# Sixteen small copies moved from SyncE's queue to ScalarE's, in a fused attention and MLP kernel with a newly written order of emission

## The chip, the cores and the metric

The kernel runs on one core of a Trainium2 chip. The metric is the device time of one execution in microseconds, as the median of several runs. The profile is one execution taken by the hardware profiler; its times are microseconds from the first instruction.

## What is computed

```python
# attention, per batch and head (B=2, H=8, S=768, D=64)
k_sum = k.reshape(B, H, 24, 32, D).max(axis=3)
v_sum = v.reshape(B, H, 24, 32, D).mean(axis=3)      # the "value sums"
scores_l = scale * q @ k.T,  kept where |i - j| < 16, else -1e9
scores_s = scale * q @ k_sum.T + log(32)
a = softmax(concat([scores_l, scores_s]))
x = a @ concat([v, v_sum])                           # 1536 tokens x 512
# first MLP: 512 -> 2048 -> 512
h = relu(x @ w_in);  y = (h * h) @ w_out
# second MLP: 512 -> 1024 -> 512
h = y @ w2_in
solu = h * softmax(h)
out = (layernorm(solu) * g_ln) @ w2_out
```

All inputs and the output are float32.

## The kernel before

The program has three parts, and their work is interleaved. The attention is cut into sixteen units: four blocks of tokens (512, 256, 256 and 512 of them) times four pairs of heads. The first MLP runs in 54 steps; a step is one product with w_in (`mm1`, line 505, twelve matmuls), a relu, squares, and one product with w_out (`mm2`, line 537, twelve matmuls). The second MLP walks over twelve row blocks (lines 587 to 647). In both MLPs every float32 operand is split into a high and a low part, and three products replace one.

The emission order is a table written out by hand, `ORDER` (lines 21 to 59). Each token names a piece of work by a letter, an index and, where it can run on several engines, a last letter for the engine: `a` is ScalarE (ACT), `d` is VectorE (DVE), `p` is GpSimd (POOL). Every engine works through its own instructions in this order, so an instruction that waits holds up those behind it on its engine. SyncE (SP) issues the DMAs, also in that order. The pieces that matter here:

- `ls` (line 236) loads the values of one pair of heads into a `kl` buffer, laid out so that each of 96 partitions holds eight neighbouring rows. `y` (line 242) adds these eight rows in three additions of 512, 256 and 128 columns. `j` (line 249) is one matmul that adds four partitions and scales: that gives the 24 value sums of each of two heads. `J` copies them from PSUM to `vs`.
- `P` (`place_vs`, line 279) is a DMA that copies a unit's sums from `vs` to partitions 96 to 119 of the unit's value window `vw`, repeated for each of its blocks of 64 tokens. `lv` (lines 266 to 272) loads the values themselves into partitions 0 to 95. There are three windows, used in turn.
- `lk` (line 190) loads keys into a `kl` buffer too. `ls` and `lk` share two `kl` buffers, which are given out in the order of the table, so a load waits until the one two places earlier in that order has been read.
- `S` (line 316) makes scores, `R` (line 337, DVE) adds the mask and takes the maximum, `E` (line 345, ACT) the exponential, `n` and `N` (lines 350 to 355) normalise, `T` (line 361) transposes, `C` copies to SBUF (`pt`), and `V` (`att_v`, line 381) multiplies by the window `vw`. `V` needs both the load `lv` and the copy `P`. `H` (line 397, ACT) and `X` (line 94, DVE) split the result into `xh` and `xl`, on which `mm1` works.
- `K`, `Q` and `w` are copies of keys, queries and key windows (line 679 on ACT, line 676 on DVE, line 557 on POOL); `m` (line 207, DVE) is the maximum over 32 keys. `a` (line 437, ACT), `b`, `c`, `d`, `e` (lines 440, 444, 451, 454, DVE), `F` and `f` (line 94) prepare a tile of weights.
- `U`, `G` and `D` are the relu, the squares and the low part of a step; `D` stands in line 94 as `gl<-r,gh`.

The DMAs of the program signal their end on eight semaphores in turn, in the order of emission, whichever engine issues them (`DMAHW0` to `DMAHW7` below), and a DMA waits for the one that had its semaphore before.

The copy as it stands in the code:

```python
src = vs[b][32 * hp:32 * hp + NSUM]
nc.sync.dma_start(out=vw[u % NVB][WK:WN, b0:b0 + nb],
                  in_=src.unsqueeze(1).to_broadcast([NSUM, nb, P]))
```

Of the kernel before, what the change touches and what calls it, by code (L numbers as in the profile page):

```python
# [26 lines left out]
d3 e3 V2 T7 E8 ls4 l5 H2 n8 F3d P4 q5 f2d k12 K12a k13 Q5a S5 N8p X2 C7a V3 w6a a4 K13a R9 q6 b4 c4 H3 lq7 w7a T8 f3p
C8a lv5 Q6d y4p X3 S6 R10 l6 lq8 E9 n9 ls5 a5 d4 e4 M0 U0a b5 c5 N9d P5 j4 J4a q7 Q7d d5 V4 lv6 G0 D0p M1 H4 X4 m6 E10
n10 T9 l7 w8a F4a U1a e5 F5a C9a S7 O0 N10p q8 lk7 lq9 R11 E11 y5d f4d f5p V5 lv7 H5 P6 Q8d j5 J5d l8 lq10 a6 a7 X5 G1
ls6 T10 C10a lv8 b6 c6 d6 e6 F6a b7 S8 R12 w9a M2 n11 P7 N11d D1d l9 q9 Q9a k14 k15 K14a K15a T11 lq11 c7 d7 e7 f6p  # L30
w10a C11d S9 R13 O1 P8 E12 n12 a8 m7 F7a q10 Q10a N12p b8 c8 d8 U2a V6 H6 X6 V7 H7 X7 ls7 lv9 l10 T12 C12d f7p lq12 G2
# [24 lines left out]
f40p b44 c44 d44 e44 O49 M51 a45 F42d b45 c45 g44 G50 D50p Ya49 Yd49 O50 g43 U51d G51 d45 e45 g45 D51d F43d f41d f42p
z0 F44a F45a M52 U52a G52 O51 Z0d a46 b46 M53 c46 d46 e46 f43d f44d f45d U53a i0 D52d O52 l47 a47 G53 b47 c47 z1 Z1d
g46 F46a D53d d47 e47 g47 F47d f46p i1 f47p z2 Z2p u0 O53 Yd53 Ya53
"""


# [697 lines left out]
```

## Time and profile before

| | before |
|---|---|
| median of 3 runs | 501.98 us (500.7 to 502.87) |
| profiled execution | 504.72 us |
| its span, first to last instruction | 503.0 us |
| mean granted TensorE clock | 0.983 |
| busy: PE / DVE / ACT / POOL | 94% / 67% / 49% / 23% |
| first matmul of the first MLP | 58.15 us |
| last of the attention's splits (`X15`) | about 155 us |

The span is divided by stage: before the first product of the first MLP (attention alone, 58 us), the stretch in which attention and first MLP are mixed (to 155 us), the first MLP with weight preparation (to about 352 us), the passage to the second MLP (to 381 us), and the second MLP. "PEclk" is the TensorE clock that was granted, as a share of 2.4 GHz. In a chain of work each line is a piece that ended last and released the next; DMA issues stand under SPq, the SyncE's queue.

### The profile page before, as it was taken

The page shows a single profiled execution, that of the slowest core. Times are in us where ns is not written, and L with a number is a line of the kernel's source. Part 1 is how long each engine was busy: PE and PEld are TensorE (multiplying, and loading weights), DVE is VectorE, ACT ScalarE, POOL GpSimd, SP SyncE. Part 2 cuts the span into 40 slices and gives each one's busy share as a digit, 9 for nine tenths or more (in the row PEclk, how much of TensorE's full clock was granted, in tenths as well). Part 3 has the DMA queues.
Part 4 walks back from the last instruction along what each step waited for, and adds up shares of the span by engine and source line. Part 5 has one row for each costly group of instructions (what it writes and reads, how often), then busy time and mean ns, then how long its engine had stood idle before and what let it go on. Part 6 is the DMA issues. An engine that isn't in the chain of part 4 may idle for free.

```text
span 503.0 us, 8088 instructions
## 1 busy us (share of the span) xinstructions
PE 473.9 (94%) x2968; PEld 394.8 (78%) x2968; DVE 339.0 (67%) x756; ACT 247.9 (49%) x576; POOL 116.9 (23%) x134
## 2 busy tenths in 40 slices
PE   3686699999999999999999999999999999999997
PEld 2465477789999888888888888888877888888886
DVE  4777889875785459345237778986778787665560
ACT  3687688777764544435326536465522332222231
POOL 3255432721321331511022302101312112110000
PEclk9788899999999999999999999999999999999999
DMA  9999886486224122333011332330000010000011
GB/s 189 206 233 201 214 206 171 98 156 137 74 60 110 51 83 87 81 94 81 36 43 42 124 124 89 125 125 1 1 1 1 22 42 22 21 22 22 21 43 42
DMA packets 60359, 44.04 MB, mean 88 GB/s; under 512 B 46624, under 2 KB 49184, under 8 KB 60320
## 3 DMA queue, kind: packets, MB, share of 16 engines
q1 hardware_dynamic: 60320, 43.53, 34.9%
q8 instruction: 23, 0.38, 0.3%
q14 instruction: 16, 0.13, 0.1%
HBM read 39.19 MB, written 3.15 MB: 84 GB/s over the span
## 4 chain that ended last, share of the span: by engine, by line
PE 78%; DVE 7%; DMA 4%; issue 4%; POOL 3%; ACT 3%; SPq 2%; POOLq 0%; DVEq 0%; ACTq 0%
PE h L505 25%; PE acc L537 23%; PE po L647 13%; PE h L587 9%; DMA kl<-in_v_dram 2%; PE lt L624 2%; PE at L316 2%; PE at L381 1%; POOL kl L242 1%; DMA qr<-in_q_dram 1%; PE at L361 1%; DVE sm L337 1%; ACT sm L345 1%; DVE wf L444 1%; POOL sm L355 1%
## 5 line engine op out<-in xcount | busy, mean ns | idle before, releaser
L505 PE MATMUL h<-xh,wi 128*128 128x512 f32 (+1 forms) x432 | 131.9, 371 | 0.0
L537 PE MATMUL acc<-gh,wo 128*128 128x512 f32 (+1 forms) x432 | 130.2, 368 | 0.0
L505 PEld LDWEIGHTS h<-xh,wi 128*128 128x128 f32 x432 | 79.3, 190 | 14.5 <-issue 0.8
L537 PEld LDWEIGHTS acc<-gh,wo 128*128 128x128 f32 x432 | 78.7, 188 | 14.3 <-issue 1.0
L505 PE MATMUL h<-xl,wi 128*128 128x512 f32 (+1 forms) x216 | 79.5, 368 | 0.0
L537 PE MATMUL acc<-gl,wo 128*128 128x512 f32 (+1 forms) x216 | 79.2, 367 | 0.2 <-DVE gl L94 0.2
L587 PE MATMUL h<-w,wf 128*128 128x512 f32 x288 | 67.4, 390 | 0.5 <-DVE st L598 0.5
L587 PEld LDWEIGHTS h<-w,wf 128*128 128x128 f32 x288 | 54.0, 188 | 11.9 <-PE lt L624 0.7
L515 ACT ACTIVATE r<-h 128x512 f32<-128x512 f32 (+1 forms) x34 | 19.0, 559 | 63.7 <-PE h L505 62.6
L94 POOL TENSOR_TENSOR gl<-r,gh 128x512 fp32r<-128x512 f32 (+1 forms) x19 | 21.5, 1131 | 117.9 <-ACT r L524 103.4
L523 ACT ACTIVATE gh<-r 128x512 fp32r<-128x512 f32 (+1 forms) x54 | 31.3, 580 | 35.0 <-DVE r L517 26.8
L537 PEld LDWEIGHTS acc<-gl,wo 128*128 128x128 f32 x216 | 40.7, 188 | 7.1 <-DVE gl L94 0.7
L505 PEld LDWEIGHTS h<-xl,wi 128*128 128x128 f32 x216 | 41.0, 190 | 6.3
L94 DVE TENSOR_TENSOR gl<-r,gh 128x512 fp32r<-128x512 f32 (+1 forms) x35 | 25.8, 738 | 23.6 <-ACT r L524 21.8
L597 ACT ACTIVATE st<-h,nm 128x1024 f32<-128x1024 f32 x12 | 13.4, 1117 | 51.1 <-DVE nm L594 51.1
L454 DVE SCALAR_TENSOR_TENSOR wf<-st,wf 128x512 uint32<-128x512 uint32 x48 | 36.5, 763 | 1.0
L345 ACT ACTIVATE sm<-sm,mn 128x120 f32<-128x120 f32 x96 | 36.5, 383 | 0.5 <-DVE mn L337 0.4
L437 ACT ACTIVATE wf<-st 128x512 f32<-128x512 f32 x48 | 31.1, 660 | 8.9 <-DMA st<-in_moe_w_in_dram 6.4
L451 DVE SCALAR_TENSOR_TENSOR wf<-st,wf 128x512 uint32<-128x512 uint32 x48 | 34.3, 718 | 1.1
L524 ACT ACTIVATE r<-r 128x512 f32<-128x512 f32 (+1 forms) x54 | 31.6, 585 | 1.8
L440 DVE TENSOR_SCALAR wf<-wf 128x512 f32<-128x512 f32 x48 | 24.8, 518 | 11.1 <-ACT wf L437 11.0
L610 POOL TENSOR_TENSOR vr<-vr,mhalf 128x1 f32<-128x1 f32 x12 | 6.6, 550 | 105.0 <-DVE vr L609 105.0
(126 smaller groups left out, 755.6 us busy)
## 6 DMA issues: line engine op xcount, KB each, us to landing
st<-in_moe_w_out_dram SPq DMA_DIRECT2D x24, 512.0 KB, 3.4
st<-in_moe_w_in_dram SPq DMA_DIRECT2D x32, 256.0 KB, 4.2
st<-in_moe_w_in_dram SPq DMA_DIRECT2D x8, 512.0 KB, 4.0
kl<-in_v_dram SPq DMA_DIRECT2D x8, 384.0 KB, 4.2
kl<-in_k_dram SPq DMA_DIRECT2D x16, 192.0 KB, 4.5
out_dram<-ob SPq DMA_DIRECT2D x11, 256.0 KB, 2.0
vw<-in_v_dram SPq DMA_DIRECT2D x16, 168.0 KB, 3.9
qr<-in_q_dram SPq DMA_DIRECT2D x16, 128.0 KB, 5.0
```

What stands on the lines that cost most here:

```text
L94: eng.tensor_tensor(out=lo, in0=x, in1=hi.bitcast(F32), op=ALU.subtract)
L345: nc.scalar.activation(out=sm[:, j], in_=sm[:, j], func=AF.Exp, bias=mn[:, j:j + 1], scale=-1.0, accum_out=su[:, j:j + 1])
L437: nc.scalar.activation(out=wf_t[n], in_=st_t[n].rearrange("p (n t) -> p n t", t=2)[:, :, 1], func=AF.Abs)
L440: nc.vector.tensor_scalar(out=wf_t[n], in0=wf_t[n], scalar1=C_LO, scalar2=C_HI, op0=ALU.max, op1=ALU.min)
L451: nc.vector.scalar_tensor_tensor(out=w, in0=st[:, :, 0], scalar=29, in1=w, op0=ALU.logical_shift_right, op1=ALU.bitwise_or)
L454: nc.vector.scalar_tensor_tensor(out=w, in0=st[:, :, 1], scalar=0xC0000000, in1=w, op0=ALU.bitwise_and, op1=ALU.bitwise_or)
L505: nc.tensor.matmul(ps[:, 0:hi - lo], wi[:, wsel, d, :], x[t][:, d, lo:hi], start=(n == 0), stop=(n == 3 * HP - 1))
L523: nc.scalar.activation(out=gh, in_=r, func=AF.Square)
L524: nc.scalar.activation(out=r, in_=r, func=AF.Square)
L537: nc.tensor.matmul(acc_t[e][:, lo:hi], wo[:, wsel, e, :], x, start=(edge(s, -1, 3) and i == 0), stop=(edge(s, 1, 3) and i == 2))
L587: nc.tensor.matmul(h2[:, fs], x[:, c, :], w_t[NW1 + nh * NDC + c][:, wsel, :], start=(n == 0), stop=(n == 3 * NDC - 1))
L647: nc.tensor.matmul(po[:, ds], x[:, cs], w_t[NW1 + 8 + c][:, wsel, ds], start=(n == 0), stop=(n == 3 * NF2 - 1))
```

## The change

The DMA of line 279 is issued from ACT's queue instead of SP's: sixteen instructions. The table `ORDER` is written anew over its whole length (its two first lines stand here for it). Nothing else differs; what is computed and the number of pieces of work are the same.

```diff
 ORDER = """
-ls0 y0d j0 J0a lk0 k0 K0d l0 lq0 lk1 a0 k1 K1d m0 q0 w0a Q0a b0 c0 d0 e0 l1 F0a a1 S0 R0 E0 lq1 lk2 R1 E1 k2 k3 q1 ls1
-K2d K3d b1 n0 m1 lq2 k4 K4a N0p c1 k5 Q1d T0 lv0 lk3 lq3 lv1 K5d m2 w1a S1 y1p w2a f0d j1 C0d J1a q2 ls2 k6 R2 P0 E2
...
+ls0 lk0 lq0 l0 y0d j0 k0 J0d ls1 k1 lk1 K0a K1a q0 Q0a m0 y1d w0a l1 lq1 a0 S0 b0 j1 R0 E0 k2 lk2 K2d k3 K3a c0 d0 ls2
+e0 n0 m1 l2 lv0 J1a a1 R1 w1a N0p T0 b1 lq2 c1 d1 e1 q1 Q1a k4 k5 K4a y2p S1 C0d F0a F1a lk3 K5d m2 E1 w2p R2 R3 j2
...
@@ place_vs, line 279
             src = vs[b][32 * hp:32 * hp + NSUM]
-            nc.sync.dma_start(out=vw[u % NVB][WK:WN, b0:b0 + nb], in_=src.unsqueeze(1).to_broadcast([NSUM, nb, P]))
+            nc.scalar.dma_start(out=vw[u % NVB][WK:WN, b0:b0 + nb], in_=src.unsqueeze(1).to_broadcast([NSUM, nb, P]))
```

Three places show what moves.

**SP's queue** before the first MLP, before the change. It begins with the third load of values for sums (`kl<-in_v_dram`) and ends with the copy of unit 1's sums (`vw_107<-vs`); `vw_108` is the window of unit 2:

```order
L236 DMA kl<-in_v_dram 96x2x512 [waits DMAHW4_49,PE_49]
L279 DMA vw_106<-vs 24x8x128 [waits DMAHW5_49,Activation_49]
L190 DMA kl<-in_k_dram 128x6x64 [waits DMAHW6_49,PE_49]
L190 DMA kl<-in_k_dram 128x6x64 [waits DMAHW7_49]
L217 DMA qr<-in_q_dram 128x2x64 [waits DMAHW0_49]
L217 DMA qr<-in_q_dram 128x2x64 [waits DMAHW1_49]
L427 DMA st<-in_moe_w_out_dram 128x1024 [waits DMAHW2_49]
L266 DMA vw_108<-in_v_dram 80x2x64 [waits DMAHW3_49]
L272 DMA vw_108<-in_v_dram 96x7x64 [waits DMAHW4_49]
L272 DMA vw_108<-in_v_dram 96x7x64 [waits DMAHW5_49]
L279 DMA vw_107<-vs 24x8x128 [waits DMAHW6_49,Activation_49]
```

The same depth with the change, from the query loads of unit 2 to the first load for unit 2's window; the load `kl<-in_v_dram` here is the fourth one:

```order
L217 DMA qr<-in_q_dram 128x4x64 [waits DMAHW5_49]
L217 DMA qr<-in_q_dram 128x4x64 [waits DMAHW6_49]
L190 DMA kl<-in_k_dram 128x6x64 [waits DMAHW7_49,PE_49]
L190 DMA kl<-in_k_dram 128x6x64 [waits DMAHW1_49]
L266 DMA vw_107<-in_v_dram 80x2x64 [waits DMAHW2_49]
L272 DMA vw_107<-in_v_dram 96x7x64 [waits DMAHW3_49]
L272 DMA vw_107<-in_v_dram 96x7x64 [waits DMAHW4_49]
L236 DMA kl<-in_v_dram 96x2x512 [waits DMAHW6_49,DMAHW0_49,PE_49]
L217 DMA qr<-in_q_dram 128x4x64 [waits DMAHW7_49]
L217 DMA qr<-in_q_dram 128x4x64 [waits DMAHW0_49]
L427 DMA st<-in_moe_w_out_dram 128x1024 [waits DMAHW1_49,DVE_49,Activation_49]
L266 DMA vw_108<-in_v_dram 80x2x64 [waits DMAHW2_49]
```

The copies have left the queue, and the fourth load of values stands ahead of the values of unit 2, where the third stood before. The second of the two `qr` loads behind it waits on `DMAHW0`, which the copy of unit 0 has had, now on ACT.

**ACT's queue** before the first MLP, before the change. It runs from the exponentials of the third group (line 345) to the copies of key tile 4:

```order
L345 ACTIVATE sm,su<-sm,mn 128x120 x4
L679 ACTIVATE qT_104<-acc_337 128x512
L679 ACTIVATE kT_97<-acc_344 128x384
L679 ACTIVATE pt<-acc_369 120x512
L679 ACTIVATE qT_105<-acc_383 128x512
L345 ACTIVATE sm,su<-sm,mn 128x120 x8
L397 ACTIVATE xh<-acc_436 128x512
L345 ACTIVATE sm,su<-sm,mn 128x120 x4
L437 ACTIVATE wf<-st 128x512
L679 ACTIVATE kT_98<-at 128x384 x2
```

With the change, from the exponentials of the second and third group to the split `xh` of unit 0:

```order
L345 ACTIVATE sm,su<-sm,mn 128x120 x8
L437 ACTIVATE wf<-st 128x512
L345 ACTIVATE sm,su<-sm,mn 128x120 x4
L279 DMA vw_106<-vs 24x8x128
L679 ACTIVATE qT_104<-acc_377 128x512
L679 ACTIVATE pt<-acc_394 120x512
L279 DMA vw_107<-vs 24x8x128
L679 ACTIVATE kT_97<-acc_433 128x384
L345 ACTIVATE sm,su<-sm,mn 128x120 x4
L679 ACTIVATE kw<-kT_97 128x8x96
L679 ACTIVATE kw<-ks_102 128x8x24
L397 ACTIVATE xh<-acc_448 128x512
```

Two copies of sums now stand between exponentials, key copies and `pt` copies.

**DVE's queue** in the mixed stretch, before the change. It runs from the end of one softmax (`su`) over key maxima (line 207) and weights to the low part of a step (`gl`):

```order
L351 RECIPROCAL su<-su 128x4
L207 TENSOR_REDUCE ks_101<-kT_96 128x24
L440 TENSOR_SCALAR wf<-wf 128x512
L444 TENSOR_SCALAR wf<-wf 128x512
L451 SCALAR_TENSOR_TENSOR wf<-st,wf 128x512
L94 TENSOR_TENSOR xl<-at,xh 128x256 x2
L676 COPY pt<-at 120x512
L94 TENSOR_TENSOR gl<-r,gh 128x512
L440 TENSOR_SCALAR wf<-wf 128x512
L454 SCALAR_TENSOR_TENSOR wf<-st,wf 128x512
L444 TENSOR_SCALAR wf<-wf 128x512
L451 SCALAR_TENSOR_TENSOR wf<-st,wf 128x512
```

With the change, about the same depth into the queue:

```order
L350 TENSOR_SCALAR su<-su 128x4
L351 RECIPROCAL su<-su 128x4
L355 TENSOR_TENSOR sm<-sm,su 128x480
L517 TENSOR_SCALAR r<-h 128x512
L676 COPY vs<-at 24x128
L440 TENSOR_SCALAR wf<-wf 128x512
L444 TENSOR_SCALAR wf<-wf 128x512
L451 SCALAR_TENSOR_TENSOR wf<-st,wf 128x512
L350 TENSOR_SCALAR su<-su 128x4
L351 RECIPROCAL su<-su 128x4
L355 TENSOR_TENSOR sm<-sm,su 128x480
L94 TENSOR_TENSOR xl<-at,xh 128x256
```

Before, the pair of lines 350 and 351 is not followed by a multiplication of line 355 on this engine (POOL has it); with the change both pairs are (`sm<-sm,su`).

## Rows read from the trace of the kernel before

**Rows 1.** Busy time by stage: us, per engine busy (instructions), clock, DMA share, GB/s.

```profile
core 0: us, PE busy (x) PEld busy (x) DVE busy (x) ACT busy (x) POOL busy (x), PEclk, DMA share, GB/s
24.60:43.40 18.80, 12.74 (x171) 10.35 (x171) 14.70 (x64) 14.07 (x52) 10.60 (x12) 0.86 1.05 228
43.40:58.20 14.80, 9.63 (x142) 7.79 (x141) 12.09 (x34) 13.00 (x43) 8.41 (x8) 0.85 0.92 188
58.20:100.90 42.70, 41.12 (x342) 31.55 (x339) 37.04 (x110) 31.88 (x94) 16.55 (x15) 0.97 0.66 167
100.90:155.00 54.10, 53.93 (x612) 49.44 (x612) 36.76 (x131) 37.54 (x126) 15.22 (x16) 1.00 0.53 107
155.00:352.00 197.00, 197.00 (x891) 163.78 (x891) 125.02 (x209) 96.27 (x164) 36.09 (x27) 1.00 0.26 81
352.00:381.00 29.00, 28.17 (x129) 22.91 (x129) 23.15 (x38) 9.37 (x16) 7.92 (x7) 1.00 0.01 1
```

**Rows 2.** Chain that ended last, 24.6 to 43.4: start us, us, what.

```profile
24.62 4.87 DMA kl<-in_v_dram
...
29.62 1.27 POOL kl L242
...
32.28 0.41 PE acc L249 x2
...
32.71 6.72 DMA kl<-in_v_dram
...
39.57 1.27 POOL kl L242
...
43.02 0.40 PE acc L249 x2
```

**Rows 3.** Waits, 0 to 58.2: engine line waited for: total us, times, longest.

```profile
ACT vs L679 <- PE acc L249: 6.9, 2, 4.9
...
PE acc L249 <- POOL kl L242: 4.8, 3, 3.0
```

**Rows 4.** PE in order of time at unit 3's values, scores and first step.

```profile
52.10 1.15 PE L381 MATMUL acc<-pt,vw 120*64 120x64 f32 x32
...
57.14 1.08 PE L316 MATMUL at<-kw,qT 64*64 64x120 f32 x16 [1.94 <-DVE qT L676]
58.15 0.79 PE L505 MATMUL h<-xh,wi 128*128 128x512 f32 x1
```

**Rows 5.** SP's queue in order of time, 24 to 43.

```profile
25.18 0.97 SPq L279 DMA_DIRECT2D vw<-vs  x1
...
38.82 0.81 SPq L279 DMA_DIRECT2D vw<-vs  x1
...
40.26 1.76 SPq L272 DMA_DIRECT2D vw<-in_v_dram  x2
```

**Rows 6.** DMA issues by kind: count, KB each, median us to landing.

```profile
vw<-in_v_dram SPq DMA_DIRECT2D x16, 168.0 KB, 3.9
```

**Rows 7.** ACT groups, 24.6 to 58.2: count, busy us, mean ns, idle before.

```profile
L679 ACT ACTIVATE pt<-acc 120x512 f32<-120x512 f32 x6 | 3.4, 590 | 1.0 <-PE acc L361 1.0
...
L679 ACT ACTIVATE kw<-kT 128x384 f32<-128x384 f32 x4 | 2.1, 530 | 0.0
...
L679 ACT ACTIVATE kw<-ks 128x96 f32<-128x96 f32 x4 | 1.2, 288 | 0.0
```

**Rows 8.** DVE groups, 58.2 to 155: the same columns.

```profile
L451 DVE SCALAR_TENSOR_TENSOR wf<-st,wf 128x512 uint32<-128x512 uint32 x12 | 8.2, 687 | 0.2
...
L355 DVE TENSOR_TENSOR sm<-sm,su 128x480 f32<-128x480 f32 x5 | 3.3, 657 | 0.1
...
L94 DVE TENSOR_TENSOR wi<-wf,wi 128x512 fp32r<-128x512 f32 x3 | 3.1, 1046 | 0.0
...
L94 DVE TENSOR_TENSOR gl<-r,gh 128x256 fp32r<-128x256 f32 x4 | 2.2, 560 | 0.5 <-ACT r L524 0.4
...
L207 DVE TENSOR_REDUCE ks<-kT 128x24 f32<-128x768 f32 x2 | 1.9, 932 | 0.0
```

More of the change, by code (lines that the diff above doesn't have):

```diff
@@ L27 @@
[L27 to L31, printed above, removed]
@@ L57 @@
[L57 to L58 removed]
+ls0 lk0 lq0 l0 y0d j0 k0 J0d ls1 k1 lk1 K0a K1a q0 Q0a m0 y1d w0a l1 lq1 a0 S0 b0 j1 R0 E0 k2 lk2 K2d k3 K3a c0 d0 ls2
+e0 n0 m1 l2 lv0 J1a a1 R1 w1a N0p T0 b1 lq2 c1 d1 e1 q1 Q1a k4 k5 K4a y2p S1 C0d F0a F1a lk3 K5d m2 E1 w2p R2 R3 j2
+J2d E2 lv1 a2 n2 n1 E3 P0 ls3 q2 N2d N1d b2 c2 Q2a n3 T1 T2 S2 C1d N3p lq3 l3 C2a d2 e2 P1 lv2 k6 R4 k7 V0 K6a T3 y3p
@@ new lines @@
+E4 lq4 K7d m3 w3a R5 H0 q3 lk4 n4 N4d l4 Q3d T4 a3 w4p X0 S3 E5 C3d b3 c3 d3 lq5 V1 C4a f0p R6 P2 lv3 n5 N5p R7 j3 J3d
+q4 lk5 k8 k9 E6 H1 T5 n6 N6d K8a K9a f1p a4 T6 X1 lq6 E7 Q4d S4 C5d b4 q5 l5 V2 e3 Q5a n7 C6a lv4 R8 N7p P3 H2 T7 E8
+F2d F3d w5p w6a X2 lq7 q6 C7d k10 Q6a k11 f2d V3 n8 K10a c4 d4 K11a e4 l6 a5 lk6 S5 R9 N8p P4 lv5 H3 E9 f3p q7 Q7d T8
+S6 X3 M0 l7 b5 c5 F4a d5 a6 ls4 e5 C8a lq8 n9 N9p R10 F5a V4 U0d w7a k12 H4 f4d M1 K12a lv6 E10 X4 T9 b6 l8 f5d P5 c6
+d6 e6 U1a S7 y4d a7 b7 M2 C9a V5 n10 lv7 c7 G0 G1 N10p lq9 R11 D0d T10 l9 q8 F6a O0 H5 d7 e7 X5 P6 U2a a8 f6p lq10
@@ new lines @@
+C10a Q8d m4 j4 lv8 D1p w8a q9 k13 m5 J4a b8 c8 d8 Q9a F7a e8 M3 K13a a9 l10 f7d G2 S8 b9 c9 q10 ls5 F8a O1 d9 e9 U3a
+R12 V6 l11 F9a E11 f8d f9d M4 n11 G3 D2d lq11 Q10a N11p T11 m6 H6 w9a X6 D3d P7 lk7 y5p S9 C11a l12 O2 E12 R13 lv9 n12
+N12d a10 j5 w10a U4d V7 J5d T12 E13 b10 q11 M5 lq12 c10 d10 lq13 H7 C12a n13 N13d a11 X7 b11 Q11d k14 P8 c11 U5a k15
+d11 ls6 K14a G4 e10 lv10 O3 e11 F10d a12 D4d ls7 f10p K15d m7 S10 q12 w11p M6 R14 Q12d G5 D5p U6a T13 S11 P9 C13d M7
+F11d y6p l13 V8 U7a O4 H8 X8 R15 f11p E14 n14 q13 G6 j6 O5 Q13d lq14 w12a N14d lv11 D6p y7p J6a P10 G7 T14 w13a V9 H9
@@ new lines @@
+C14d M8 Yd5 lq15 S12 X9 U8d w14p V10 Ya5 R16 a13 lv12 M9 l14 H10 E15 X10 j7 O6 D7d E16 n15 N15d J7a O7 R17 b12 c12 U9a
+lv13 n16 G8 N16d q14 T15 G9 M10 Q14a C15a D9p D8d P11 b13 P12 T16 S13 d12 e12 U10a C16d E17 O8 R18 R19 E18 M11 n17
+N17d V11 U11d O9 n18 N18d H11 X11 P13 c13 T17 d13 M12 l15 C17d G10 G11 D10p a14 U12d T18 e13 w15a V12 H12 D11d C18d
+M13 E19 X12 S14 U13d O10 lv14 lv15 R20 n19 E20 O11 R21 N19p T19 n20 N20d q15 C19a M14 Q15a G12 T20 G13 D12d S15 E21
+l16 U14d C20d O12 D13d R22 a15 n21 E22 V13 N21d b14 c14 G14 M15 d14 P14 n22 a16 R23 N22p O13 U15d H13 D14d b15 X13 O14
@@ new lines @@
+G15 e14 E23 c15 T21 l17 d15 M16 e15 D15d C21a n23 P15 T22 N23d U16a V14 G16 C22d D16p T23 M17 C23d H14 X14 V15 b16 l18
+U17a c16 a17 O15 d16 H15 X15 O16 b17 G17 c17 e16 M18 d17 l19 e17 D17p O17 U18a G18 M19 Yd17 Ya17 l20 D18d O18 F12d
+f12d F13a U19d G19 M20 f13p a18 b18 a19 D19d c18 O19 d18 U20a b19 G20 c19 e18 d19 l21 e19 M21 D20d F14d f14p F15a a20
+O20 F16a F17d f15d U21a G21 f16d l22 F18d a21 b20 D21d M22 f17d O21 c20 d20 U22a G22 e20 l23 a22 D22d M23 b22 b21 c21
+d21 e21 O22 a23 l24 U23a b23 c22 G23 d22 M24 e22 D23d F19d f18d f19d F20a O23 F21a U24d G24 lg0 D24p M25 F22d c23 d23
@@ new lines @@
+e23 l25 O24 U25d f20d G25 l26 a24 D25d M26 b24 c24 d24 e24 a25 b25 O25 F23d c25 d25 U26d a26 l27 f21d G26 M27 f22d
+D26p O26 U27d a27 e25 G27 b26 l28 c26 D27d M28 O27 U28d f23p G28 a28 D28p M29 b27 c27 O28 U29d d26 G29 e26 d27 l29 M30
+e27 D29p O29 U30a G30 D30d l30 M31 Yd29 Ya29 a29 b28 O30 U31d G31 D31d M32 O31 U32a G32 M33 c28 b29 c29 d28 e28 l31
+D32d O32 d29 e29 U33d G33 D33d M34 l32 O33 U34d G34 M35 U35a D34p O34 G35 D35p M36 O35 U36d G36 M37 Ya35 Yd35 D36p O36
+F24d f24d F25a U37a G37 f25p M38 F26a D37p a30 a31 f26p O37 b30 a32 c30 b31 U38a c31 G38 d30 e30 M39 b32 F27a l33 d31
@@ L59 @@
+D47p b43 b42 O47 a44 c42 d42 U49a c43 G48 d43 e42 g41 e43 l45 M50 D48d O48 F40a F41a b44 c44 G49 g42 U50a d44 e44 l46
+f39d D49p O49 G50 f40d f41p g43 g44 F42d M51 D50p Yd49 l47 F43a F44a Ya49 a45 a46 U51a f42p O50 f43d f44d G51 b46 b45
+c45 a47 d45 e45 M52 D51p g45 F45a z0 f45d O51 Z0p U52a c46 d46 e46 M53 G52 D52p g46 F46d b47 c47 d47 i0 U53a e47 G53
+z1 D53p O52 g47 F47a f46d f47p i1 z2 Z2d Z1d O53 u0 Yd53 Ya53
 """
```

33 lines of the change are left out of this document (5 added, 28 removed).

## The prediction

> **What bounds the kernel now.** I read the busy time by stage first [rows 1]. From 100.9 us on PE is busy 53.93 of 54.10, 197.00 of 197.00 and 28.17 of 29.00 us: these stages cost what their matmuls cost, at a granted clock of 1.00 (2.4 GHz), and an order of emission takes nothing from them. From 58.2 to 100.9 PE is idle for 1.6 us and its clock is 0.97. What can be won lies before the first product of the first MLP: from 24.6 to 58.2 PE is busy for 22.4 of 33.6 us, at a clock of 0.86 and 0.85. None of the other engines is full there either: DVE 26.8, ACT 27.1.
>
> So something is waited for, and the chain of work that ended last says what [rows 2]. Between 24.6 and 43.4 it is nearly all one thing: a load of values for the sums (4.87 us), the additions on POOL (the first of three takes 1.27 us), two sum matmuls, the next load into the freed buffer (6.72 us), the additions, two matmuls. The list of waits agrees [rows 3]: PE stood 4.8 us for the additions on POOL, and ACT 6.9 us for sum matmuls whose result it was to copy. The first step of the MLP comes at 58.15 [rows 4], right behind scores that had waited 1.94 us for queries from DVE; the product of unit 3's values, which completes the first input of the MLP, stands at 52.10.
>
> SP's copies of sums take 0.97 and 0.81 us each to issue [rows 5], and while SP waits for the sums, what is behind them in its queue waits too: behind the third copy stand the values of unit 3, last issued at 40.26 plus 1.76 us. Values take 3.9 us to land [rows 6], so these were there at about 45.9, and used at 52.10: 6.2 us of slack.
>
> **The change, part by part.** *Start, up to the first step.* In the new order the loads for the sums stand earlier (the fourth where the third was), one of the early additions goes from POOL to DVE, and SP no longer waits at the copies. The chain of [rows 2] should therefore end earlier than other work. What is late next is DVE: in 24.6 to 43.4 it is busy for 14.70 of 18.80 us [rows 1], and its work ahead of the first step stays nearly what it was (four copies of keys and two maxima leave; three copies of `pt`, two multiplications, two small copies of sums and one set of additions come). With the chain gone, the stretch shrinks at most to its DVE time: 18.80 − 14.70 = 4.1 us. That lies near PE's 4.8 us for POOL. The bounds are 0 (another chain, by the transfers, ends at the same moment; DMA is at 1.05 there) and about 7: the 6.2 us of slack of unit 3's values and the 0.81 us of the copy ahead of them on SP. I take 4.1, since DVE's row is the nearest resource in the same stretch.
>
> *The copies on ACT.* Five of them come before the first step; at the mean of 0.97 and 0.81 [rows 5] that is 5 × 0.89 = 4.4 us on ACT's queue, if issuing on ACT takes as long as on SP, which this trace does not show. In turn four `pt` copies of 0.59 and three pairs of key-window copies of 0.53 and 0.29 [rows 7] leave ACT there, 4.8 us, and of the small ones about as much comes as goes. So ACT's load stays, with 6.5 us idle in 33.6 [rows 1]: 0, with bounds of −1 and +4.4 (nothing hidden). In the mixed stretch eleven more copies, 9.8 us, meet 27.4 us of idle ACT time (96.8 − 31.88 − 37.54): 0.
>
> Here is a rule that bears on the first term. These rows give 0.8 to 1.0 us for an issue against 3.9 us to landing. The Trainium skill ("DMA: Bandwidth & Descriptors", section "Issuing engines are not separate DMA queues") says that DMAs run on the same engines whoever starts them, and that starting them from several engines saves only the sequencer's time to start them, usually small relative to the DMA itself. By that rule the first term is at most the five issues, an estimate of 4.4 us from the issue rows, and its upper bound of 7 us falls. The trace agrees on the sizes (0.8 to 1.0 against 3.9 us); what a wait in front of an issue costs, which the rule leaves out, no run here shows yet.
>
> *Mixed stretch, 58.2 to 155.* DVE receives work: ten multiplications instead of five (0.657 each, 3.3 us), three low parts more (0.56, 1.7), two low parts of weights (1.05, 2.1), two key maxima (0.93, 1.9), four passes over weights of which the dear kind takes 0.69 (2.5) [rows 8], and two relus, three copies, and a softmax's small work, some 3 us: about 14.5 in all. POOL gets that much lighter. Idle on DVE are 5.7 us in the first stage and 17.3 in the second [rows 1], so by the sum it fits: 0. The bounds are −2 (PE's idle 1.6 + 0.2 us and the clock) and +6 (rival below).
>
> *Passage and rest.* From 352 to 381 PE is idle for 0.8 us; the new order moves weight copies there between ACT and DVE and low parts to POOL, whose waits nobody stands behind as long as the first MLP is full: 0, bounds ±1.
>
> *Sum:* −4.1 against the profiled execution of 504.72 us (span 503.0): 500.6. This execution lies 2.7 us above the median of the runs, 501.98. Against the median: 501.98 − 4.1 = **497.9 us**. About 0.5%, 2.5 us, is what a measurement of this kernel can tell from no change.
>
> **The rivals.** *R1, the start stays as long.* A DMA waits for the one eight places earlier, which had its semaphore, whoever issued it. In the new order query loads on SP wait for the copy on ACT in just this way, so SP stands for the sums still, only a few DMAs later; and the bytes ahead of unit 3's values are the same, at a DMA share of 1.05 [rows 1]. For it: the transfers of 4.87 and 6.72 us in the chain [rows 2] are long because of those others. Against it: 6.2 us of slack behind them. Then −1 at most: about 501.
>
> *R2, DVE becomes the bound of the mixed stretch (slower).* Between the first step and the seventh, DVE gets 5.5 of the 14.5 us. It is busy 37.04 of the 42.70 us in that stage [rows 1]; with 5.5 more, 42.5, it is full, and if it keeps the idle share that it has now (13%, from waits for others), the stage grows to 42.5/0.87 = 48.9, by 6.2 us. It decides as soon as the multiplications on DVE are late for the transposes. The DVE work ahead of unit 3's `xl` also grows by some 2.5 us, so the start gains only 1.6. Together +4.6: about 506.5. For it: the sum itself leaves 0.2 us. Against it: PE had 41.12 of 42.70 there, and order as well as PE's stock of steps lets DVE run late for a while.
>
> *R3, the start gains in full.* If DVE's idle time shrinks too, because it was due to the same chain, the start is bounded by unit 3's values alone: −7, about 495. For it: the granted clock of 0.85 stands beside PE's gaps here, and is 0.97 and 1.00 where there are none; 22.4 us of matmuls at 1.00 would be 3 us shorter still. Against it: DVE 14.70 of 18.80.
>
> *R4, ACT stands at the copies (slower).* On ACT a copy waits for the DMA eight earlier, and behind it stand exponentials, keys and `pt`. At 1.5 us of waiting for each of five copies (well under the 3.9 us to landing) that is 7.5 us against 6.5 us idle, and with 4.4 us of issuing ACT is the new bound of the start: +1 to +4, about 504.5. Against it: SP issued sixteen DMAs in the 13.6 us between the first two rows of [rows 5], so the one eight places earlier is some 6.8 us old when a copy comes, and lands after 3.9.
>
> **How the numbers follow.** The forecast has a chance of 0.38; R1 0.22, R2 0.15, R3 0.15, R4 0.10. Faster by over 0.5% (below 499.5) are the forecast and R3: 0.53. Within 0.5%: R1, 0.22. Slower (above 504.5): R2 and R4, 0.25, R4 lying on the border. The range goes from 491.0 (R3 with the clock's 3 us and a little of the mixed stretch) to 507.0 (R2). The cases of the faster sign alone span 491 to 499.5.
>
> **What would show it.** Right: the first step at about 54 us; no pair of a load of values and additions on POOL in the chain between 24 and 43; ACT's copies at 0.8 to 1.0 us without waits; PE full from the first step to 155, in as many us as now. Wrong: scores or transposes that wait for DVE after the first step, the line 355 among their releasers (R2); query loads on SP that wait while ACT stands at line 279 (R1, R4); a first step at 58 as now (R1) or at 51 (R3).

## The result and the profile after

The changed kernel takes 506.7 us (median of 5 runs, 505.05 to 508.42) against 501.98: a ratio of means of 1.0094, 95% interval 1.0065 to 1.0122. It is 4.7 us slower; the forecast was 4.1 us faster, 497.9.

The profiled execution of the change took 505.05 us, the shortest of its runs, and that of before 504.72, which is 2.7 us over its median. The two traces differ by 0.3 us, the medians by 4.7. So the traces alone don't tell where the time went, and the experiments below are needed for it; a second profile of before stands among them.

By stages, the changed kernel, in the columns of [rows 1]:

```profile
24.60:43.40 18.80, 13.62 (x172) 11.27 (x172) 17.73 (x73) 13.20 (x52) 7.85 (x11) 0.73 0.97 194
43.40:58.20 14.80, 8.31 (x140) 6.42 (x139) 14.39 (x40) 10.34 (x37) 5.75 (x6) 1.00 0.82 177
58.20:100.90 42.70, 42.70 (x336) 33.44 (x334) 39.75 (x109) 31.12 (x84) 15.24 (x14) 1.00 0.90 201
100.90:155.00 54.10, 53.12 (x637) 48.52 (x636) 41.18 (x150) 39.67 (x135) 12.16 (x14) 1.00 0.39 96
155.00:352.00 197.00, 194.97 (x874) 161.40 (x873) 130.03 (x211) 90.22 (x153) 42.84 (x30) 1.00 0.25 78
352.00:381.00 29.00, 28.18 (x128) 22.89 (x126) 22.70 (x36) 8.67 (x14) 6.57 (x6) 1.00 0.00 1
```

Four things have changed. From 24.6 to 43.4 us DVE is busy for 17.73 of 18.80 us, against 14.70: in the start it is now the engine that is full. From 58.2 to 100.9 PE has lost the 1.6 us of idle time that it had (42.70 of 42.70, against 41.12): that is a gain. After 100.9 PE is idle for 1.0 us. And from 155 to 352 us, where PE had no idle time, it now has 2.0 us of it (194.97 of 197.00).

Ahead of the first step DVE, with PE, PEld, ACT and POOL beside it in the columns of [rows 1], has worked as follows in the kernel before and in the changed one:

```profile
0.00:58.15 58.15, 34.76 (x413) 26.86 (x413) 42.46 (x150) 39.07 (x129) 26.84 (x52) 0.87 1.05 205
```

```profile
0.00:57.71 57.71, 32.62 (x408) 25.90 (x408) 47.15 (x157) 35.50 (x120) 22.84 (x49) 0.88 0.99 199
```

It now has 157 instructions and 47.15 us of work there, against 150 and 42.46; ACT has 3.6 us less.

PE in the changed kernel in order of time at the start, with the idle time before an instruction and what ended it:

```profile
28.00 1.93 PE L361 MATMUL acc<-ident,sm 128*120 128x128 f32 x8 [2.29 <-DVE sm L355]
...
37.42 0.62 PE L361 MATMUL acc<-ident,sm 128*120 128x128 f32 x4 [2.87 <-ACT sm L345]
...
56.23 0.41 PE L225 MATMUL at<-ident,qr 128*128 128x128 f32 x2 [2.66 <-DMA qr<-in_q_dram]
...
57.71 0.50 PE L505 MATMUL h<-xh,wi 128*128 128x512 f32 x1
```

The first step comes at 57.71, where [rows 4] have 58.15. The longest waits are now for DVE's normalising (28.00), exponentials (37.42) and queries (56.23). The chain that ended last, at the same places:

```profile
26.74 1.12 DVE sm L355 x2
...
34.92 1.46 DVE su L350
...
47.29 4.46 DMA vw<-vs
...
52.18 0.41 SPq L217
...
52.63 3.46 DMA qr<-in_q_dram
```

The pair of a value load and additions on POOL that filled [rows 2] between 24 and 43 us is gone. In its place stand DVE's work, and at the end a copy of sums (`vw<-vs`, 4.46 us from issue) behind whose landing SP issues the queries, which take 3.46 us more.

Two further places, behind 150 us, cost PE time. The last product of the attention, and two steps of the first MLP:

```profile
153.00 1.24 PE L381 MATMUL at<-pt,vw 120*64 120x64 f32 x32 [0.98 <-DVE wf L444]
```

```profile
306.37 0.50 PE L505 MATMUL h<-xh,wi 128*128 128x512 f32 x1 [0.69 <-ACT r L515]
...
318.89 0.50 PE L505 MATMUL h<-xh,wi 128*128 128x512 f32 x1 [1.35 <-DVE r L517]
```

The releaser of the first row is no input of that product; experiment v15 shows what was waited for there.

### The profile page after: what moved, and what is told of

It reads as the page before. It is cut to its first block, busy times and chain, and to the rows that moved or that the text cites. A ratio compares the mean times of both kernels' runs of the same rounds, so it can differ in the third digit from the quotient of the medians.

```text
span 503.3 us, 8086 instructions
## 1 busy us (share of the span) xinstructions
PE 471.2 (94%) x2968; PEld 393.1 (78%) x2968; DVE 356.1 (71%) x781; ACT 239.4 (48%) x556; POOL 113.9 (23%) x129
## 4 chain that ended last, share of the span: by engine, by line
PE 78%; DVE 10%; issue 5%; DMA 3%; ACT 3%; POOL 1%; SPq 0%; DVEq 0%; POOLq 0%; ACTq 0%
PE h L505 24%; PE acc L537 23%; PE po L647 13%; PE h L587 9%; PE lt L624 2%; PE at L381 2%; PE at L316 2%; DMA kl<-in_v_dram 2%; PE at L361 1%; DVE wf L454 1%; DVE wf L444 1%; DMA vw<-vs 1%; DVE sm L337 1%; DVE wf L440 1%; DVE wf L451 1%
## 5 line engine op out<-in xcount | busy, mean ns | idle before, releaser
L94 POOL TENSOR_TENSOR gl<-r,gh 128x512 fp32r<-128x512 f32 (+1 forms) x24 | 32.3, 1347 | 139.5 <-ACT r L524 104.7
L515 ACT ACTIVATE r<-h 128x512 f32<-128x512 f32 (+1 forms) x31 | 17.2, 555 | 48.3 <-PE h L505 44.5
L454 DVE SCALAR_TENSOR_TENSOR wf<-st,wf 128x512 uint32<-128x512 uint32 x48 | 39.2, 821 | 1.1
L451 DVE SCALAR_TENSOR_TENSOR wf<-st,wf 128x512 uint32<-128x512 uint32 x48 | 35.5, 740 | 1.2
L517 DVE TENSOR_SCALAR r<-h 128x512 f32<-128x512 f32 (+1 forms) x23 | 14.2, 619 | 30.2 <-PE h L505 29.9
L94 DVE TENSOR_TENSOR gl<-r,gh 128x512 fp32r<-128x512 f32 (+1 forms) x30 | 20.1, 671 | 15.2 <-ACT r L524 11.9
```

The costliest lines, as they stand in the source:

```text
L94: eng.tensor_tensor(out=lo, in0=x, in1=hi.bitcast(F32), op=ALU.subtract)
L451: nc.vector.scalar_tensor_tensor(out=w, in0=st[:, :, 0], scalar=29, in1=w, op0=ALU.logical_shift_right, op1=ALU.bitwise_or)
L454: nc.vector.scalar_tensor_tensor(out=w, in0=st[:, :, 1], scalar=0xC0000000, in1=w, op0=ALU.bitwise_and, op1=ALU.bitwise_or)
L515: nc.scalar.activation(out=r_t[s], in_=h_t.pop(s), func=AF.Relu)
```

## The experiments

Each time is the median of its runs, each ratio is one of means, to runs of before that were timed with it on the same chip (a difference of two medians from different chips is therefore less sure than one of two ratios). "New" and "old" mean the order of the change and that of before. In h1 and h2 line numbers are lower by one.

**The queue and the order, one at a time.** e1 has the new order with the copies on SP, e2 the old order with the copies on ACT:

```diff
 place_vs, in e1 from the changed kernel, in e2 from before
-            nc.scalar.dma_start(...)     # e1
+            nc.sync.dma_start(...)
-            nc.sync.dma_start(...)       # e2
+            nc.scalar.dma_start(...)
```

> The changed order, with the sixteen copies back on SP's queue. Theory L (the start gains nothing because SP still waits for each copy's landing through the eight semaphores, wherever it was issued): within 1.5 us of the changed kernel, so 505 to 508 us. Rival A (the copies cost ACT its time): 2 to 4 us faster than the changed kernel, 502.5 to 504.5. Rival Q (freeing SP's queue did help, and the order cost more than the measured 4.7 us): 508 to 511.

Measured: 506.98 us, ratio 1.0089 (1.0056 to 1.0122). With the new order the queue makes no difference that can be measured.

> The order of before, with only the sixteen copies moved to ACT's queue. Theory L: within 1.5 us of before (500.5 to 503.5), because the DMAs behind the copies wait for the same landings. Rival A: 2 to 4 us slower, 504 to 506, and ACT shows idle time in front of its work at the copies. Rival Q: 2 us or more faster, below 500.

Measured: 507.24 us, ratio 1.011 (1.0073 to 1.0147), beyond what rival A gave. The mechanism of A fails all the same: issuing holds ACT up for little of the time that it takes. In the changed kernel, ACT and its queue (ACTq) in order of time:

```profile
25.78 1.40 ACTq L279 DMA_DIRECT2D vw<-vs  x1
...
25.88 0.64 ACT L437 ACTIVATE wf<-st 128x512 f32<-128x512 f32 x1
...
142.74 0.82 ACTq L279 DMA_DIRECT2D vw<-vs  x1
143.66 0.69 ACT L437 ACTIVATE wf<-st 128x512 f32<-128x512 f32 x1 [0.56 <-issue]
```

The first issue takes 1.40 us on the queue, but an activation starts 0.10 us after it does. Behind the second one the next activation starts only when the issue is over, and ACT has idled for 0.56 us. In the trace of the changed kernel ACT's next instruction starts while the issue runs at eight of the sixteen copies; at the other eight ACT is idle behind it, but for only some 1.1 us in all was nothing else awaited (2.5 us in e2), of about 13 us of issuing.

What the traces show as a loss in e2 is when the issue comes. In the old order these copies stand on ACT behind a step's relu and squares; before, SP issued the copies of the same two units at 112.52 and 115.16. In e2:

```profile
129.39 1.65 ACTq L279 DMA_DIRECT2D vw<-vs  x2
```

```profile
132.11 1.15 PE L381 MATMUL at<-pt,vw 120*64 120x64 f32 x32 [1.78 <-DMA vw<-vs]
```

Two copies leave from 129.39 on, and PE stands 1.78 us for one of them at 132.11. From its first step (58.47) to its last product PE is idle for 4.2 us in e2, against 1.75 us in the mixed stretch of [rows 1]. That is 2.4 of the 5 us; where the rest lies was not found.

**The order cut at X15.** X15 is the last split of the attention, at 154 to 157 us.

```diff
 h1: ORDER
+the changed kernel's tokens up to X15, then what is left in the order and on the engines of before
 h2: ORDER, copies on SP
+the tokens of before up to X15, then what is left in the order and on the engines of the changed kernel
```

> The changed kernel up to the last split of the attention (X15); all pieces that are left then follow in the order and on the engines of before. Theory T (2.4 us of the loss lie behind 155 us, at 306 and 318 us, where PE waits for relus, one of them behind DVE passes that take 1.4 instead of 0.43 us while POOL works): 504.3 us, and no idle time of PE between 200 and 345 us. Without T: 506.7 as the changed kernel.

> The kernel before up to X15 (copies on SP); all pieces that are left then follow in the order and on the engines of the changed kernel. Theory T: 2.4 us slower than before, 504.4 us, with PE idle for some 2 us between 300 and 325 us. Without T: 502.0, and the whole loss would be in the start and the mixed stretch.

Measured: h1 505.39 us, ratio 1.0055 (1.0031 to 1.0079); h2 504.65 us, ratio 1.0041 (1.0015 to 1.0067). h1 came 1.1 us above the forecast, h2 within 0.3. Busy time from 200 to 345 us (columns as above) of before, the changed kernel, h1, h2 in turn:

```profile
200.00:345.00 145.00, 145.00 (x640) 119.77 (x639) 91.49 (x153) 70.99 (x120) 24.91 (x19) 1.00 0.28 85
```

```profile
200.00:345.00 145.00, 142.97 (x630) 117.74 (x629) 94.22 (x150) 63.54 (x109) 33.97 (x24) 1.00 0.23 77
```

```profile
200.00:345.00 145.00, 145.00 (x641) 119.78 (x640) 91.58 (x154) 70.70 (x119) 25.46 (x19) 1.00 0.29 88
```

```profile
200.00:345.00 145.00, 142.97 (x630) 117.76 (x629) 94.07 (x150) 63.52 (x108) 33.97 (x24) 1.00 0.24 77
```

Whoever has the new order behind X15 has 2.03 us of idle PE there, whoever has the old one has none. That part of the loss is settled: about 2 us by the ratios (2.1 in h2, 2.0 between the changed kernel and h1) as by the traces. The rest lies ahead of X15.

**Two low parts on POOL.** At the second of the two places the trace shows what was late. POOL, and DVE in the same time, in the changed kernel:

```profile
312.40 1.69 POOL L94 TENSOR_TENSOR gl<-r,gh 128x512 fp32r<-128x512 f32 x1 [4.89 <-issue]
314.05 3.17 POOL L94 TENSOR_TENSOR w<-wf,w 128x512 fp32r<-128x512 f32 x2
```

```profile
314.67 1.41 DVE L440 TENSOR_SCALAR wf<-wf 128x512 f32<-128x512 f32 x1
316.11 1.40 DVE L444 TENSOR_SCALAR wf<-wf 128x512 uint32<-128x512 uint32 x1
317.54 0.69 DVE L451 SCALAR_TENSOR_TENSOR wf<-st,wf 128x512 uint32<-128x512 uint32 x1
318.15 0.68 DVE L517 TENSOR_SCALAR r<-h 128x512 f32<-128x512 f32 x1
```

The relu of step 47 (line 517), for which PE waits 1.35 us, stands on DVE behind weight passes, and two of these (lines 440 and 444) take 1.41 and 1.40 us while POOL works on two low parts of weights; the third comes back to 0.69 once POOL is done. t2 gives these two to DVE:

```diff
-... f37p ... f38p ...
+... f37d ... f38d ...
```

> The changed kernel with the low parts of two weights (f37, f38) on DVE instead of POOL. Theory C (DVE's passes take 1.4 us instead of 0.43 while POOL works on these two; the relu of step 47 on DVE comes late for that alone, and PE stands 1.35 us at 318 us): the passes at about 0.43 us, no wait of PE for line 517, and 1.35 us faster than the changed kernel, 505.3. Rival (DVE's queue is too long there in any case): DVE has 1.4 us more to do, the wait stays or grows, 506.5 to 508.

The same two passes of DVE in t2, and the stretch from 200 to 345 us:

```profile
320.45 0.43 DVE L440 TENSOR_SCALAR wf<-wf 128x512 f32<-128x512 f32 x1
320.92 0.43 DVE L444 TENSOR_SCALAR wf<-wf 128x512 uint32<-128x512 uint32 x1
```

```profile
200.00:345.00 145.00, 144.31 (x637) 119.20 (x636) 91.97 (x152) 63.33 (x107) 30.75 (x22) 1.00 0.25 80
```

The passes take 0.43 us and PE's idle time falls from 2.03 to 0.69 us, which is the wait at 306.37, where the new order sets two first products (M45, M46) next to each other with one relu between them. So the mechanism holds in the trace. The times, 506.3 us and 1.0079 (1.0047 to 1.0111), are too wide to show 1.35 us.

The Trainium skill ("SBUF — State Buffer", section "SBUF: two separate sides") says that DVE and GpSimd share a pair of ports to SBUF: a DVE operation in a two-port mode, or with two inputs in SBUF while GpSimd's operation reads SBUF, and a GpSimd operation take it as a lock for the whole instruction, and whichever comes second waits. The trace agrees: 0.43 us alone, 1.41 beside POOL.

**The last copy.**

```diff
-... lv14 lv15 R20 ... n23 P15 T22 ...
+... lv14 lv15 P15 R20 ... n23 T22 ...
```

> The changed kernel with the copy of the last unit's sums (P15) moved forward, to right behind that unit's values (lv15); all else as in the changed kernel. Theory V (the copy is issued only 5.9 us before the product that needs it and lands among weight loads, so PE stands at the last product, 0.98 us in one trace and 2.14 us in another, and then runs at the lower clock for a while): no idle time of PE before the last product of line 381, and 1 to 2.5 us faster than the changed kernel, 504.2 to 505.7. If V is wrong: 506.7 and the same idle time.

Measured: 505.4 us, ratio 1.0064 (1.004 to 1.0089). The last product in v15, and in h1, where the copy is late and the wait was longest:

```profile
152.71 1.15 PE L381 MATMUL at<-pt,vw 120*64 120x64 f32 x32
```

```profile
154.97 2.07 PE L380 MATMUL at<-pt,vw 120*64 120x64 f32 x32 [2.14 <-DVE wf L450]
```

```profile
154.90:157.20 2.30, 2.23 (x33) 2.15 (x34) 0.00 (x0) 0.13 (x1) 0.00 (x0) 0.50 0.03 7
```

In v15 nothing is waited for. Of all traces with the new order ahead of X15, the five with the late copy (changed kernel, e1, h1, t2 and p3) have a wait of 0.93 to 2.14 us in front of this product, and the nine with the early copy none. So it is the copy. In h1 the granted clock is 0.50 (1.2 GHz) behind the wait, the product takes 2.07 instead of 1.15 us, and both are lost. In t2 and p3 (waits of 2.02 and 2.08 us) the clock falls to the same level just behind the product; in the changed kernel and e1 (0.98 and 0.93 us) it stays at 1.00. By the medians the gain is 1.3 us here, and 1.6 from h1 to k2 below; by the ratios it is 1.5 and 1.3.

**The copy of unit 3's sums.** The chain above ends with this copy and the queries behind it. p3 moves it forward:

```diff
-... j3 J3d q4 ... N7p P3 H2 ...
+... j3 J3d P3 q4 ... N7p H2 ...
```

> The changed kernel with the copy of unit 3's sums (P3) moved forward, to right behind the copy of the sums out of PSUM (J3). Theory L (a load of queries on SP stands behind this copy's landing, eight DMAs later, and the first step behind those queries; the trace shows 4.46 us of copy and 3.46 us of queries in the chain before the first step): the first step at 55 to 56.5 instead of 57.7 us, and 1 to 2 us faster than the changed kernel, 504.7 to 505.7. Rival D (DVE sets the start, 17.73 of 18.80 us busy from 24.6 to 43.4): first step at 57 to 58 as before, 506 to 507.

Measured: 509.16 us, ratio 1.0132 (1.0089 to 1.0175), with the first step at 58.55. It is not faster, against theory L; by the medians it is 2.5 us slower than the changed kernel, but the intervals overlap. ACT in p3 in order of time, and DVE's copy of the sums:

```profile
38.69 0.57 ACT L679 ACTIVATE pt<-acc 120x512 f32<-120x512 f32 x1
42.19 0.79 ACTq L279 DMA_DIRECT2D vw<-vs  x1
43.03 0.39 ACT L345 ACTIVATE sm<-sm,mn 128x120 f32<-128x120 f32 x1 [3.77 <-POOL sm L355]
```

```profile
41.86 0.30 DVE L676 COPY vs<-acc 24x128 f32<-24x128 f32 x1
```

The copy now comes up on ACT before its sums are in `vs` (41.86 plus 0.30). It leaves at 42.19, and ACT is idle for 3.77 us with exponentials and key copies behind it. PE's wait of 2.66 us for queries is down to 0.32 in this trace, and ACT's has come in its place. k1 has this edit, the early last copy, and the old order behind X15:

> The changed kernel up to X15 with both copies (P3 and P15) moved forward, and the pieces behind X15 in the order and on the engines of before. If V, L and T all hold and add up: 505.4 for the new head with the old tail, less 1 to 2.5 and less 1 to 2, so 501 to 503.4, level with before (501.98). If only V and T hold: 503 to 504.4. If neither copy matters: 505.4.

Measured: 503.94 us, ratio 1.0035 (1.0012 to 1.0059), as if only V and T held. k2 is the same without moving P3:

> The changed kernel up to X15 with only the last copy (P15) moved forward, and the pieces behind X15 in the order and on the engines of before. Theories V and T together take 1.3 (last copy alone) and 2.35 us (behind X15) from 506.7: 502.0 to 503.2, within 1.3 us of before, with no gain of the start left over. If the new start were a gain of its own: below 500.5.

Measured: 503.81 us, ratio 1.003 (1.0006 to 1.0055). So with both late losses taken away the new order still costs 1.5 us by the ratio, and nothing of the forecast gain is left over. Of P3 alone, k1 against k2, the times show nothing. In k2 PE is never idle from its first step (59.08) to the end of the first MLP, so the remainder lies ahead of the first step. The start must even have lost more than 1.5 us, an estimate of 3.3, since PE's 1.6 + 0.2 us of idle time in the mixed stretch of [rows 1] are gone in k2.

**Before, once more.**

> The kernel before, unchanged, for a second profile. Theory E (the profiled execution from which the prediction was made, 504.72 us, had a start 2 to 3 us longer than is usual for this kernel): first step at 56 to 57 instead of 58.15 us, and the time of this execution near the median of 501.9, with the same stage behind 172 us. Rival (its extra time lay elsewhere): first step at 58 again.

Measured: 500.86 us, one execution. First step, the chain that ended last at the places of [rows 2], and the first stage of [rows 1]:

```profile
55.47 0.50 PE L505 MATMUL h<-xh,wi 128*128 128x512 f32 x1
```

```profile
24.52 5.02 DMA kl<-in_v_dram
...
32.77 6.10 DMA kl<-in_v_dram
...
42.32 0.40 PE acc L249 x2
```

```profile
24.60:43.40 18.80, 12.96 (x176) 10.69 (x176) 14.54 (x64) 13.54 (x49) 11.17 (x12) 0.86 1.07 227
```

The same program has its first step at 55.47 instead of 58.15 [rows 4]; it ends 3.8 us earlier by its span, and has gained all of that by 83 us. So far theory E is right. But the surplus is not where the forecast read its first term. From 24.6 to 43.4 DVE is busy for 14.54 us here and 14.70 in [rows 1], and the chain of [rows 2] is here too, with its last sum matmuls at 42.32 instead of 43.02. The other 2.0 us to the first step arise behind this chain: there lines 440 and 444, ahead of the last scores, take 1.30 and 0.83 us beside POOL's additions in the first trace and 0.42 and 0.43 in b2. The first step itself and what follows it add 1.2 us: from 58.2 to 63.0 the granted clock is 0.75 in the first trace and 1.00 in b2.

h2, which has the old order ahead of X15 and the same queue, has its first step at 56.11. The new order has it at 57.71, 57.59 (e1), 58.14 (h1), 58.46 (v15) and 59.08 (k2). So in these traces the new start comes 1.5 to 3.6 us later than in b2 and h2, not 4.1 earlier; the first trace of before, at 58.15, is as late as they are. A safer mark is a later step, ahead of which PE has done the same matmuls in both orders. The 21st step begins, in b2 and in k2:

```profile
165.04 0.39 PE L505 MATMUL h<-xh,wi 128*128 128x512 f32 x1
```

```profile
167.03 0.39 PE L505 MATMUL h<-xh,wi 128*128 128x512 f32 x1
```

Of the 3.6 us at the first step 2.0 are left there: the rest is won back in the mixed stretch.

**What sets the new start.** In the trace of the changed kernel small DVE operations are stretched here too. DVE, and POOL beside it:

```profile
34.84 1.54 DVE L350 TENSOR_SCALAR su<-su 128x4 f32<-128x4 f32 x1
```

```profile
35.09 1.26 POOL L94 TENSOR_TENSOR wi<-wf,wi 128x512 fp32r<-128x512 f32 x1
```

An addition on 128x4 elements takes 1.54 us. The nine operations of line 350 ahead of the first step take 3.9 us in all, against 1.7 before. c2 moves three low parts from POOL to DVE, on top of k2:

```diff
-... f0p ... f1p ... f3p ...
+... f0d ... f1d ... f3d ...
```

> As k2_last_copy_early_old_tail, with the low parts of three weights (f0, f1, f3) on DVE instead of POOL. Theory C at the start (DVE is the bound there, and small operations and weight passes that stand beside POOL's low parts take 1.36 to 1.63 us instead of 0.16 to 0.69): DVE gets 3 times 0.68 us more and loses 1.38, 1.08 and 1.6 us of stretching, net 2 us less, and the first step comes 1 to 2 us earlier than in k2; 500.5 to 502. Rival: DVE's queue grows by 2 us and the start with it, 503 to 504.5.

Measured: 503.32 us, ratio 1.0018 (0.9992 to 1.0043), first step at 58.49. By the medians that is half a microsecond in the right direction, less than the times can tell; in the traces the 21st step comes at 168.02, 1.0 us later than in k2. The stretching itself is gone (line 350: 1.4 us for the same nine operations), but with the low parts DVE is busy for 46.36 us ahead of the first step, against 46.10 in k2. c3 has the early copy P3 as well:

> As c2_and_low_parts_of_start_on_dve, with the copy of unit 3's sums (P3) moved forward as in p3_fourth_copy_early. Theory B (two bounds end together before the first step: queries behind that copy's landing, and DVE stretched by POOL; each edit alone only uncovers the other): the first step at 56 to 57.5, and 1 us or more faster than either k1 (503.9) or c2 (503.3), 501.5 to 502.5. Rival D (DVE alone, in the amount of its work): first step at 58.3 to 59, 503 to 504.

Measured: 503.6 us, ratio 1.0055 (1.0036 to 1.0073), first step at 59.60. Theory B falls; the early copy holds ACT up here too (it leaves at 42.98, while ACT's last work ended at 39.13). d2 leaves POOL alone and gives three copies back to ACT, on top of k2:

```diff
-... C0d ... C1d ... C3d ...
+... C0a ... C1a ... C3a ...
```

> As k2_last_copy_early_old_tail, with three early copies of transposed weights to SBUF (C0, C1, C3) on ACT, where the kernel before had most of them, instead of DVE. Theory D (the new order takes work from ACT to make room for copies whose issue hardly holds ACT up, and gives it to DVE, which is the bound with 17 to 18 of 18.8 us busy): 2 us less on DVE, the first step 0.5 to 2 us earlier than in k2 (59.08), 502 to 503.3. Rival A (ACT has no room beside the copies): same or later, 503.8 to 505.

Measured: 502.31 us, ratio 1.002 (1.0 to 1.0041). PE in d2:

```profile
55.07 0.41 PE L225 MATMUL at<-ident,qr 128*128 128x128 f32 x2 [2.48 <-DMA qr<-in_q_dram]
...
57.03 0.79 PE L505 MATMUL h<-xh,wi 128*128 128x512 f32 x1
```

The first step comes 2.05 us earlier than in k2, but at the 21st step (166.15) only 0.9 us of that are left; DVE is busy for 45.16 us ahead of the first step, against 46.10. The time is 1.5 us lower by the medians and 0.5 by the ratios, and the intervals overlap. So trace and times point to theory D without showing it. With P3 moved as well (d3):

> As d2_three_pt_copies_on_act, with the copy of unit 3's sums (P3) moved forward. Theory B with D: both bounds moved away, the first step at 55.5 to 57, 500.5 to 502. If only DVE counts: as d2 within 0.7 us. If only the queries count: as k1, 503.9.

Measured: 503.49 us, ratio 1.0054 (1.0035 to 1.0073), first step at 60.61: no gain again. d4 takes the wait for queries that d2 still has (2.48 us) off the path by moving the queries instead of the copy, and d4s puts the copies on SP:

```diff
-... f3p q7 Q7d T8 S6 X3 M0 ...
+... f3p T8 S6 X3 M0 q7 Q7d ...
```

> As d2_three_pt_copies_on_act, with the transposes and the copy of unit 7's queries (q7, Q7) moved behind the first step M0, which doesn't need them. Theory L2 (in d2 PE waits 2.48 us at 55 us for these queries, whose load on SP stands behind the landing of unit 3's copy, and unit 8's transposes, scores and the first step stand behind them on PE): that wait is gone, the first step comes at 55 to 56 instead of 57.03 us, and 1 to 2 us faster than d2 (502.3): 500.3 to 501.3, level with before or a little under. If another engine is late too (DVE with the split of unit 3): first step at 57, 502.3.

> As d4_query_transposes_behind_first_step, with the sixteen copies on SP's queue. If the queue matters once the order is mended: 1 us or more slower than d4. If it doesn't, as e1 against the changed kernel showed: within 0.7 us of d4.

Measured: d4 507.51 us, ratio 1.0098 (1.006 to 1.0135); d4s 506.99 us, ratio 1.0088 (1.0054 to 1.0123). PE in d4:

```profile
57.53 0.78 PE L505 MATMUL h<-xh,wi 128*128 128x512 f32 x1
...
65.80 0.55 PE L199 MATMUL at<-ident,kl 128*128 128x128 f32 x3 [2.24 <-DVE mn L337]
```

DVE in d4, its copy of these queries:

```profile
62.40 0.42 DVE L676 COPY qT<-at 128x256 f32<-128x256 f32 x1 [4.97 <-PE at L225]
```

The first step comes at 57.53. The transposes of the queries now stand behind its twelve matmuls on PE, so DVE waits 4.97 us for them at their copy, with weight passes and maxima behind it, and at 65.80 PE waits 2.24 us for those maxima. The stall was moved behind the first step and became dearer. d4s lies 0.5 us from d4, so the queue makes no difference here either.

One candidate for a better kernel was the old order with two early low parts moved from POOL to DVE:

```diff
-... f1p ... f3p ...
+... f1d ... f3d ...
```

> The kernel before with the low parts of two weights (f1, f3) on DVE instead of POOL. Theory C: in the trace with the head of before, POOL's second one (1.73 us at 52.4) runs beside DVE's own low part, which takes 1.48 instead of 0.69; DVE gets 1.4 us more and loses 0.8: no change, 501 to 503. Rival: an engine that is slowed twice over is worth freeing, 499 to 500.5.

Measured: 505.39 us, ratio 1.004 (1.0007 to 1.0073), slower, though its own profiled execution (500.61 us) was among the fastest here. Its twelve times leave a gap: three lie from 500.61 to 501.17, nine from 504.5 to 505.89. Its one trace is of the first three, with the first step at 55.16, so it cannot tell why the others are slower. No version beat the kernel before.

## Why the prediction was wrong

**The sum's first term failed, "18.80 − 14.70 = 4.1 us", and in it the step "its work ahead of the first step stays nearly what it was".** The term took DVE's busy time of before as what is left once the chain is gone. In the new start DVE is busy for 17.73 us in that stretch, and for 47.15 us ahead of the first step against 42.46 (41.53 in b2). The pieces that it listed as going and coming give only some 1.2 us more by their durations in the trace of before. It left out that more passes over weights stand ahead of the first step (16 of lines 440, 451 and 454, against 13), and it took durations from rows of before, where other pairs of operations had met: line 350 alone takes 3.9 us instead of 1.7. Its own R2 put the growth of DVE's work ahead of unit 3's `xl` at some 2.5 us; the forecast did not use that. How much of the late start each of the two makes stays open: d2, which gives three copies back to ACT, is 0.9 us faster in the trace and 0.5 to 1.5 by the times, with overlapping intervals, and no experiment brought the start down to that of b2. So that DVE holds the new start is argued from its load, not shown.

**The base was not what failed.** The term was read from one execution that lay 2.7 us above its median, and the text noted that and carried the 4.1 over to the median. b2 shows the same stretch with nearly the same numbers: the sum would have been 18.80 − 14.54 = 4.3 us there.

**The chain of value sums did go**, as forecast, and DVE and the queries took its place. That the queries stand behind a copy's landing is the mechanism of R1, and it is seen in the chain. It was not the only bound: none of the edits that took it away (p3, k1, c3, d4) gained time.

**ACT's copies were costed right for a wrong reason.** The forecast hid 4.4 us of issuing behind 4.8 us of work removed. The issues need little cover, since ACT loses some 1.1 us at all sixteen. The removed work went to DVE, where it did harm, as far as d2 tells. R4, ACT standing at a copy, did not occur in the changed kernel, where each copy is issued within 0.3 us of the start of the instruction before it; p3 shows what it looks like, 3.77 us of idle ACT in one place.

**"Mixed stretch: 0" was too careful up to 150 us and failed behind it.** PE is busy for 42.70 of 42.70 us in its first stage, so the 1.6 us of idle time that were the term's lower bound were in fact won. R2 expected DVE to be late for PE here, so that R2's 506.5 us lies next to the measured time is chance; of R2 only the growth of DVE's work in the start came true. The last product behind a late copy, 1.3 to 1.6 us by the times, was in no term: the copies were counted as issues, and when each lands before its product was not looked up for the late ones.

**The stages behind 155 us had no term for a loss.** The passage itself held: from 352 to 381 PE is idle for 0.8 us in both traces. But "an order of emission takes nothing from them" was read as if an order could add nothing either. Between 200 and 345 us there are 2.0 us of idle PE, of which 1.35 come from two low parts on POOL next to DVE's weight passes and 0.69 from two adjacent first products. A relu on DVE stands in the same queue as the weights, and the next step behind it.

By the ratios the last copy is worth 1.5 us (changed kernel to v15), the order behind X15 1.7 (v15 to k2), and 1.5 us are left for the start less what the mixed stretch won (k2); these make up the 4.7 us by their construction. h2, which has the old order ahead of X15, gives 2.1 us for the second part on its own. Each is uncertain by over a microsecond.

## What to carry to other kernels

A stretch shrinks to an engine's busy time only if that time is counted anew for the new program: every piece that comes and goes, and with durations from rows in which the same pairs of operations meet. A second profile of the same program tells which part of a stall is there each time: here the chain was, and the first step still moved by 2.7 us. When an order takes work from an engine to make room for DMA issues, see first whether issues hold that engine up at all, and where the work goes. Where two engines slow each other, a queue that a full TensorE waits on (here relus on DVE) needs its durations from rows in which both run.

## What was not expected of the hardware

The issue of a copy takes 0.79 to 1.40 us on ACT's queue, and at half of the copies ACT's next instruction starts before the issue is over (0.10 us after its start in one place), at the other half only behind it. DVE operations of 0.16 to 0.43 us took 1.40 to 1.54 us beside a POOL operation on 128x512 elements. And executions of the same program differ by 3.8 us in their first 83 us (504.72 and 500.86), but by less than 0.1 us from 200 us on to the end.
